# Fewer zeroed rows ahead of the scatters, a hold on weight tiles, and a free bank for the last attention round

## The chip, the cores and the metric

The kernel runs on one core of one Trainium2 chip. The metric is device time in microseconds (us) of one execution, as the median of several runs. The core has five engines that run their own instruction streams and wait for one another through semaphores: TensorE (PE in the profile, with its weight loads as PEld), VectorE (DVE), ScalarE (ACT), GpSimd (POOL) and SyncE (SP, which here only issues DMAs). ACT and POOL issue DMAs too.

## The reference

Three layers follow one another on 1536 tokens of width 384, all in float32:

```
state, per head, over 768 time steps:
    y_t = r_t (state + (u k_t) v_t);  state = w * state + k_t v_t      # 2 x 8 heads of width 48
x = y as 1536 tokens x 384
expert_idx = argmax(x @ w_gate)            # 8 experts, at most 384 tokens each, in token order
out[i] = gate_w[i] * (relu(x[i] @ w1[e]) @ w2[e])      # w1[e]: 384 x 1024, w2[e]: 1024 x 384
return (sigmoid(x @ w_gate2) * (x @ w_val)) @ w_out    # width 1536 between
```

## The kernel before

**Stage 1, attention.** Eight rounds `s` (four head pairs of two batches) run on PE, DVE, ACT and POOL. Round s does the output sums of its last two token blocks, transposes its result, and prepares rounds s+1 to s+3. `y_in` and `y_own` add up a round's outputs in PSUM, `out_evac` copies them to SBUF on ACT, `out_tr` transposes them on PE, `out_x` takes the transposed tokens and the gate's logits. For round 7, `y_in` takes one PSUM tile of two banks and calls its halves y7[0] and y7[1].

**Stage 2, routing.** `r1a` to `r3c` find each token's expert and its rank in it, for batch 0 during rounds 3 to 5 and for batch 1 after round 7. `r3c` writes gate weights behind each token's row and has POOL scatter the rows by six indirect DMAs per batch into a DRAM buffer `xs_d`, 1536 rows per expert (L228). The kernel works on NB = 224 rows of an expert at a time, so rows behind an expert's count are read too and must be finite: `zinit` (L663) writes zeros from SBUF over the first 224 rows of all eight experts, three DMAs in round 3 and five in round 4, on SP's queue. The first weight tile `raw[0]` is made to wait for all eight (`zl`, L140), so that it doesn't compete with them. Expert 0's rows of batch 0 come back by `pre()`; the rest of expert 0 is picked out of SBUF by matmuls in `first()`.

**Stage 3, experts.** 64 steps i = 8e + f. `s1(e, f)` multiplies expert e's tokens by a slice of w1, `s2` by a slice of w2, three steps later. Weight tiles of 384 KB come by `fetch` on SP into five buffers `raw`; `bg` splits each into a rounded part `rh` (ACT, L151) and the rest `rl` (DVE, L153). `eload(e)` brings expert e's 224 rows from `xs_d`: expert 1 at i = 0 on POOL's queue, expert 2 at i = 9 and expert 3 at i = 15 on SP's, the others at f = 7. `escale(e)` scales them on ACT (L939), `etr` transposes them on PE (L948). For expert 1 that is at i = 7 and 8, for expert e > 1 at f = 3 and f = 4, 6 of the expert before. `c1` (i = 9) sums the experts' counts on PE and DVE; `c3` loads offsets into registers. `dfetch` brings the tiles of stage 4's weights, 768 KB each, on SP.

**Stage 4**, the gated layer, is 48 steps of matmuls on the sorted tokens; its results are scattered to the output.

The order on every engine is the order in which the code calls these functions. Every engine, and the queue of DMAs that it issues, goes in order: an instruction that waits holds what is behind it. DMAs carry semaphores in rotation, eight for those of SP (DMAHW0 to 7) and eight for those of POOL (DMASW0 to 7), and a DMA also waits until the last one with its own semaphore has landed.

Of the kernel before, what the change touches and what calls it, by code (L numbers as in the profile page):

```python
# [32 lines left out]
WG = 5  # L33
ZI = (0, 0, 0, 3, 5, 0, 0, 0)
NKR = 3
# [79 lines left out]
def body(tc, A, out):  # L115
    nc = tc.nc
    E = mybir.EngineType
    with ExitStack() as top, tc.manual_schedule():
        gp_ = top.enter_context(tc.tile_pool(name="gp", bufs=1))
        rp_ = top.enter_context(tc.tile_pool(name="rp", bufs=NRAW))  # L120
        dr = top.enter_context(tc.tile_pool(name="dr", bufs=1, space=DRAM))
        xs_d = dr.tile([8 * 1536, XW], F32, tag="xs_d", name="xs_d")
        ids_d = dr.tile([1536, 1], I32, tag="ids_d", name="ids_d")
# [9 lines left out]
        def fetch(n):  # L133
            while nxt[0] < n:
                m = nxt[0]
                nxt[0] += 1
                raw[m] = rpl[0].tile([128, 768], F32, tag="raw", name="raw", bufs=rpl[1])
                i = nc.sync.dma_start(out=raw[m], in_=A["wx"][m // 2][:, (m % 2) * 768:(m % 2) * 768 + 768])
                if m == 0 or m == sum(BG) + 1:
                    after(i, xr0l if m else zl)  # L140

# [82 lines left out]

        scx, sci, sco, xr0l, zl = [], [], [], [], []

# [30 lines left out]
        mxi = gp_.tile([1, 1], I32, tag="mxi", name="mxi")  # L257
        one8 = gp_.tile([128, 8], F32, tag="one8", name="one8")
        cpos = gp_.tile([128, 12], I32, tag="cpos", name="cpos")
        with ExitStack() as ctx:  # L260
# [185 lines left out]
            def y_in(s):  # L446
                if s == 7:
                    y7t = ps.tile([128, 2, 512], F32, tag="a", name="y7")
                    for g in range(2):
                        y7[g] = y7t[:, g, :]  # L450
                else:
                    Y0[s] = pb.tile([128, 512], F32, tag="big", name="y0")
                T1[s] = pb.tile([128, 512], F32, tag="big", name="t1")
                for c in ((1, 4, 5, 2, 3) if s == 7 else (1, 2, 3, 4, 5)):
                    t = ts[s % 2].rearrange("q (d c) -> q d c", c=5)[:, :, c - 1]
                    for h in range(2):
                        q = slice(64 * h, 64 * h + 48)
                        nc.tensor.matmul(y_out(s, c)[64 * h:64 * h + 64], t[q], D[s][q, 0, c * 128:(c + 1) * 128],
                                         start=c in (1, 4) or s == 7 and c == 2, stop=False, skip_group_check=True)
# [125 lines left out]
            def first():  # L585
# [27 lines left out]

                nc.vector.tensor_scalar(out=keep, in0=rank, scalar1=capf, scalar2=None, op0=ALU.is_lt)
                choose(0)
                for c in range(6):
                    low(c)
                    if c < 5:
                        choose(c + 1)
                    if c == 0:  # L620
                        r3c(1)
                xk = [pb.tile([128, 512], F32, tag="big", name="xk")[:, 0:NB] for _ in range(3)]
# [29 lines left out]
            def consts():  # L652
# [6 lines left out]
                nc.gpsimd.tensor_copy(out=capf, in_=capi)  # L659

            zi = [0]

            def zinit():  # L663
                e = zi[0]
                if e < 8:
                    zi[0] += 1
                    zl.append(nc.sync.dma_start(out=xs_d[e * 1536:e * 1536 + NB, :].rearrange("(b p) d -> p b d", p=NP),
                                                in_=zero[0:NP]).ins)

# [66 lines left out]
            for s in range(8):  # L736
# [7 lines left out]
                fetch(sum(BG[:max(s + 2, 4)]) if s else 0)  # L744
                for _ in range(ZI[s]):
                    zinit()
                if s == 2:
# [10 lines left out]
                if nx:  # L758
# [3 lines left out]
                    if s == 6:  # L762
                        bg(1, False, 0, None, nc.vector.tensor_copy)
                    out_x(s, s == 6)
# [20 lines left out]
                if s == 6:  # L785
                    a_cp(7, C1, ap1)
                    bg(BG[s] - 2, False, 0, subs)
                    bg(1, False, 0, subs, nc.vector.tensor_copy)
                    cnt(0)
                    for f in subs:  # L790
                        f()
                if nx:
                    y_in(s + 1)
# [40 lines left out]
        with ExitStack() as ctx:  # L834
# [6 lines left out]
            def c1():  # L841
# [90 lines left out]
            def eload(e, eng=nc.sync):  # L932
                xr[e] = mp.tile([128, 2, XW], F32, tag="xr", name="xr")
                after(eng.dma_start(out=xr[e][0:NP], in_=xs_d[e * 1536:e * 1536 + NB, :].rearrange("(b p) d -> p b d", p=NP)), scx)

# [67 lines left out]
            for i in range(64 + LAG):  # L1003
                if i == OVP:
                    overflow()
                if i < 64:
# [142 lines left out]
```

## Time and profile before

| | |
|---|---|
| median of 3 runs | 452.23 us (450.78 to 454.71) |
| the profiled execution | 452.19 us, of which the instructions span 450.4 |
| PE busy | 432.6 us, 96% of the span |
| DVE, ACT, POOL busy | 63%, 50%, 24% |
| TensorE's granted clock, mean | 0.988 of full speed |

The profile counts an engine as busy while an instruction runs; a matmul's end is modelled, so that a busy PE is not PE at its peak. Waits are put down to the engine or DMA that released them last. Line numbers are those of the kernel before.

### The profile page before, as it was taken

How to read it: one execution, taken by the hardware profiler on the slowest of the kernel's cores; microseconds unless marked ns; L12 is line 12 of the kernel's file. 1: busy time of each engine (PE TensorE's matmuls, PEld its weight loads, DVE VectorE, ACT ScalarE, POOL GpSimd, SP SyncE). 2: the span in 40 equal slices, each digit the busy share in tenths (PEclk: the TensorE clock that was granted, in tenths of full speed). 3: DMA queues.
4: the chain of work that ended last, by engine and by line, in shares of the span. 5: the costliest groups of instructions: out<-in, count | busy, mean ns of one | idle time of the engine just before them, and what ended most of it. 6: DMA issues, size and time to landing. Idle time of an engine off the chain costs nothing.

```text
span 450.4 us, 8284 instructions
## 1 busy us (share of the span) xinstructions
PE 432.6 (96%) x3214; PEld 413.1 (92%) x3215; DVE 283.7 (63%) x496; ACT 224.3 (50%) x489; POOL 106.0 (24%) x102
## 2 busy tenths in 40 slices
PE   8999988969999999999999999999999999999994
PEld 4788876959999999999999999999999999999993
DVE  6888978727899899984677877778531222212211
ACT  5587765627787778763544444344352212222132
POOL 2466753300010112030035453232122000000013
PEclk9999999979999999999999999999999999999998
DMA  7999976754988886775026352340011000000002
GB/s 241 332 276 236 307 260 209 265 165 146 332 284 251 281 277 191 229 139 179 0 71 140 72 140 87 124 141 1 1 53 54 1 1 0 1 0 1 1 17 87
DMA packets 23194, 63.02 MB, mean 140 GB/s; under 512 B 4656, under 2 KB 8400, under 8 KB 23152
## 3 DMA queue, kind: packets, MB, share of 16 engines
q1 hardware_dynamic: 20992, 57.36, 43.0%
q0 software_dynamic: 2016, 5.10, 3.1%
q8 instruction: 26, 0.43, 0.4%
q14 instruction: 16, 0.13, 0.1%
q10 hardware_dynamic: 144, 0.00, 0.0%
HBM read 54.92 MB, written 7.53 MB: 139 GB/s over the span
## 4 chain that ended last, share of the span: by engine, by line
PE 72%; DMA 16%; ACT 4%; DVE 3%; issue 2%; POOL 1%; SPq 1%; POOLq 0%; DVEq 0%; ACTq 0%
PE pg L1072 17%; PE pv L1072 16%; PE po L1097 16%; PE ph L966 8%; PE py L985 7%; PE py L984 4%; DMA xs_d<-zero 4%; DMA kt<-in_kr_dram 3%; DMA raw<-in_wx_dram 3%; DMA dm<-in_dm_dram 3%; ACT rh L151 2%; DMA xr<-xs_d 1%; DMA xs_d<-xs,pi 1%; PE xp L948 1%; ACT xr L939 1%
## 5 line engine op out<-in xcount | busy, mean ns | idle before, releaser
L1082 DVE TENSOR_TENSOR sg<-sg,pv 128x384 f32<-128x384 f32 (+2 forms) x49 | 26.6, 543 | 79.5 <-PE pv L1072 79.5
L153 DVE TENSOR_TENSOR rl<-raw,rh 128x768 fp32r<-128x768 f32 x61 | 61.2, 1004 | 15.1 <-ACT rh L151 14.9
L985 PE MATMUL py<-hh,rh 128*128 128x448 f32 x192 | 65.1, 381 | 0.0
L1083 ACT CAST gh<-sg 128x384 fp32r<-128x384 f32 (+2 forms) x49 | 24.8, 507 | 78.1 <-DVE sg L1082 78.0
L1084 DVE TENSOR_TENSOR gl<-sg,gh 128x384 fp32r<-128x384 f32 (+2 forms) x49 | 35.6, 727 | 28.9 <-ACT gh L1083 28.9
L984 PE MATMUL py<-hh,rl 128*128 128x224 f32 x192 | 53.4, 278 | 0.0
L197 POOL TENSOR_TENSOR wy<-wa,wy 128x768 fp32r<-128x768 f32 x10 | 19.9, 1992 | 140.1 <-ACT wy L193 140.1
L1078 ACT ACTIVATE sg<-pg 128x384 f32<-128x384 f32 x48 | 23.5, 490 | 58.8 <-PE pg L1072 58.6
L151 ACT CAST rh<-raw 128x768 fp32r<-128x768 f32 x62 | 51.4, 832 | 1.8 <-DMA raw<-in_wx_dram 1.8
L968 ACT ACTIVATE hh<-ph 128x224 fp32r<-128x224 f32 x64 | 22.9, 358 | 34.0 <-PE ph L966 33.7
L228 POOL DMA_INDIRECT out_dram<-ob,ids x12 | 11.7, 975 | 118.0 <-ACT ob L1104 115.6
L985 PEld LDWEIGHTS py<-hh,rh 128*128 128x128 f32 x192 | 37.1, 193 | 2.2
L984 PEld LDWEIGHTS py<-hh,rl 128*128 128x128 f32 x192 | 37.6, 196 | 0.0
L1097 PE MATMUL po<-wy,gh 128*128 128x384 f32 x144 | 36.7, 335 | 0.0
L969 DVE SCALAR_TENSOR_TENSOR hh<-ph,hh 128x224 fp32r<-128x224 f32 x64 | 24.6, 385 | 10.4 <-ACT hh L968 9.9
L413 ACT ACTIVATE at<-cst,dl 128x128 f32<-128x128 f32 x88 | 27.2, 389 | 5.7 <-DVE dl L399 4.8
L966 PE MATMUL ph<-xh,rh 128*128 128x224 f32 x96 | 26.4, 275 | 0.4 <-DVE hh L969 0.4
L966 PE MATMUL ph<-xl,rh 128*128 128x224 f32 x96 | 26.5, 276 | 0.0
L966 PE MATMUL ph<-xh,rl 128*128 128x224 f32 x96 | 26.3, 274 | 0.0
L966 PE MATMUL ph<-xeh,rh 128*128 128x224 f32 x96 | 26.1, 274 | 0.0
L966 PE MATMUL ph<-xeh,rl 128*128 128x224 f32 x96 | 26.1, 275 | 0.0
L1097 PEld LDWEIGHTS po<-wy,gh 128*128 128x128 f32 x144 | 26.0, 188 | 0.0
(206 smaller groups left out, 1188.2 us busy)
## 6 DMA issues: line engine op xcount, KB each, us to landing
raw<-in_wx_dram SPq DMA_DIRECT2D x64, 384.0 KB, 4.6
r<-in_wy_dram SPq DMA_DIRECT2D x18, 768.0 KB, 4.9
kt<-in_kr_dram SPq DMA_DIRECT2D x7, 576.0 KB, 10.1
dm<-in_dm_dram SPq DMA_DIRECT2D x5, 672.0 KB, 10.4
xs_d<-zero SPq DMA_DIRECT2D x8, 339.5 KB, 7.2
v<-in_v_dram SPq DMA_DIRECT2D x8, 288.0 KB, 10.8
xr<-xs_d SPq DMA_DIRECT2D x6, 339.5 KB, 7.4
dm<-in_dm_dram SPq DMA_DIRECT2D x6, 288.0 KB, 11.6
```

Of the source, the lines that this page charges most:

```text
L151: cast(out=h, in_=t)
L153: (nc.gpsimd if pool else nc.vector).tensor_sub(rl[n % NR], t, h.bitcast(F32))
L413: nc.scalar.mul(AT[s][:, j, :], ident, DL[s][:, j:j + 1])
L966: nc.tensor.matmul(ph, a[:, w], b[:, kt, :], start=(i == 0), stop=(i == 8))
L969: nc.vector.scalar_tensor_tensor(out=h[:, 1, :], in0=ph, scalar=0.0, in1=h[:, 0, :].bitcast(F32), op0=ALU.max, op1=ALU.subtract)
L984: nc.tensor.matmul(y[:, 0, :], wl[:, w], h[:, 0, :], start=(f == 0), stop=False, skip_group_check=True)
L985: nc.tensor.matmul(y, wh[:, w], h, start=False, stop=(f == 7), skip_group_check=True)
L1072: nc.tensor.matmul(pg[g], w[a][:, q], x[b][:, kt, :], start=(kt == 0 and (a, b) == (0, 0)), stop=(kt == 2 and b == 1))
L1082: nc.vector.tensor_mul(gg[:, a:b], sg[:, a:b], pg[1][:, a:b])
L1083: nc.scalar.copy(out=gh[:, a:b], in_=gg[:, a:b])
L1084: nc.vector.tensor_sub(gl[:, a:b], gg[:, a:b], gh[:, a:b].bitcast(F32))
L1097: nc.tensor.matmul(po[i], g[v][:, a], w[u][:, q], start=(f == 0 and (u, v) == (0, 0)), stop=(f == 11 and v == 1))
```

## The change

- **Zeros.** `zinit` is gone. In round 3 four DMAs write zeros: over the rows of experts 0, 1 and 2, and into a new DRAM buffer `z_d` of 224 rows. Each of 112 partitions now writes two rows that lie together. `raw[0]` waits for no zeros.
- **Clearing later.** `c1` works out, for each expert whose count n is under 224, the row 1536e + n, else a row behind the buffer (which is 224 rows longer). At steps 11, 12, 13, 14 and 16 `clear(e)` for e = 3 to 7 loads that row into a register of POOL and copies `z_d` there, DRAM to DRAM, on POOL's queue.
- **Raw tiles held.** The tile with m = XG = 9 waits until expert 1's rows have landed (`xr1l`).
- **Round 7.** y7[1] is the bank that held the `ups` sums, so the two halves lie in two tiles. In round 6 all four of the round's `raw` casts stand ahead of `out_x` (one on DVE, three on ACT, where it was two and two), and the first subtraction with them.
- **`r3c(1)`** stands ahead of the first `choose`, no longer behind the second.

```
-        xs_d = dr.tile([8 * 1536, XW], F32, tag="xs_d", name="xs_d")
+        xs_d = dr.tile([8 * 1536 + NB, XW], F32, tag="xs_d", name="xs_d")
+        z_d = dr.tile([NB, XW], F32, tag="z_d", name="z_d")
...
-                if m == 0 or m == sum(BG) + 1:
-                    after(i, xr0l if m else zl)
+                if m in (sum(BG) + 1, XG):
+                    after(i, xr1l if m == XG else xr0l)
...
-                    y7t = ps.tile([128, 2, 512], F32, tag="a", name="y7")
-                    for g in range(2):
-                        y7[g] = y7t[:, g, :]
+                    y7[0] = ps.tile([128, 2, 512], F32, tag="a", name="y7")[:, 0, :]
+                    y7[1] = ud_ps
...
+                r3c(1)
                 choose(0)
                 for c in range(6):
                     low(c)
                     if c < 5:
                         choose(c + 1)
-                    if c == 0:
-                        r3c(1)
...
-                for _ in range(ZI[s]):
-                    zinit()
+                if s == 3:
+                    for z in [xs_d[e * 1536:e * 1536 + NB, :] for e in range(ZS)] + [z_d]:
+                        nc.sync.dma_start(out=z.rearrange("(p b) d -> p b d", b=2), in_=zero[0:NP])
...
                     if s == 6:
-                        bg(1, False, 0, None, nc.vector.tensor_copy)
+                        bg(1, False, 0, subs, nc.vector.tensor_copy)
+                        bg(BG[s] - 1, False, 0, subs)
+                        subs.pop(0)()
                     out_x(s, s == 6)
...
                 if s == 6:
                     a_cp(7, C1, ap1)
-                    bg(BG[s] - 2, False, 0, subs)
-                    bg(1, False, 0, subs, nc.vector.tensor_copy)
-                    cnt(0)
                     for f in subs:
                         f()
+                    cnt(0)
...
+                nc.vector.scalar_tensor_tensor(out=zo, in0=cf[0:1, :], scalar=-12288.0, in1=e1536, op0=ALU.add, op1=ALU.add)
+                nc.vector.scalar_tensor_tensor(out=zo, in0=cf[0:1, :], scalar=float(NB), in1=zo, op0=ALU.is_lt, op1=ALU.mult)
+                nc.vector.tensor_scalar_add(zoi, zo, 12288.0)
                 nc.vector.reduce_max(out=mxi, in_=cf[0:1, :], axis=AX.X)
+
+            def clear(e):
+                r = nc.values_load(zoi[0:1, e:e + 1], engines=[E.Pool], min_val=0, max_val=8 * 1536,
+                                   skip_runtime_bounds_check_because="behind an expert's rows")
+                nc.gpsimd.dma_start(out=xs_d[bass.ds(r, NB), :], in_=z_d)
...
+                    if i in ZE:
+                        clear(ZE[i])
```

with `ZS = 3`, `ZE = {11: 3, 12: 4, 13: 5, 14: 6, 16: 7}` and `XG = 9`.

SP's queue from the last `v` tile of attention (round 4) to the first tiles of stage 3, before the change. `dm<-xs_d` is `pre()`:

```order
L302 DMA v<-in_v_dram 128x576 [waits DMAHW3_49,PE_49]
L667 DMA xs_d<-zero 112x2x388 [waits DMAHW4_49]
L667 DMA xs_d<-zero 112x2x388 [waits DMAHW5_49]
L667 DMA xs_d<-zero 112x2x388 [waits DMAHW6_49]
L667 DMA xs_d<-zero 112x2x388 [waits DMAHW7_49]
L667 DMA xs_d<-zero 112x2x388 [waits DMAHW0_49]
L138 DMA raw<-in_wx_dram 128x768 [waits DMAHW5_49,DMAHW4_49,DMAHW6_49,DMAHW2_49,DMAHW7_49,DMAHW1_49,DMAHW0_49]
L138 DMA raw<-in_wx_dram 128x768
L138 DMA raw<-in_wx_dram 128x768 [waits DMAHW3_49]
L138 DMA raw<-in_wx_dram 128x768 x2
L581 DMA dm_124<-xs_d 112x2x388 [waits DMASW3_49,DMASW2_49,DMASW4_49,DMASW1_49,DMASW5_49,DMASW0_49,DVE_49]
L138 DMA raw<-in_wx_dram 128x768 [waits DMAHW6_49,DMAHW1_49,DVE_49]
```

and in the changed kernel, from the same `v` tile on:

```order
L308 DMA v<-in_v_dram 128x576 [waits DMAHW4_49,PE_49]
L141 DMA raw<-in_wx_dram 128x768 [waits DMAHW5_49]
L141 DMA raw<-in_wx_dram 128x768 [waits DMAHW6_49]
L141 DMA raw<-in_wx_dram 128x768 [waits DMAHW7_49]
L141 DMA raw<-in_wx_dram 128x768 [waits DMAHW0_49]
L141 DMA raw<-in_wx_dram 128x768 [waits DMAHW1_49]
L586 DMA dm_127<-xs_d 112x2x388 [waits DMASW3_49,DMASW4_49,DMASW2_49,DMASW5_49,DMASW1_49,DMAHW2_49,DMASW0_49,DVE_49]
L141 DMA raw<-in_wx_dram 128x768 [waits DMAHW3_49,DMAHW5_49,DMAHW2_49,DVE_49]
L141 DMA raw<-in_wx_dram 128x768 [waits DMAHW6_49,DMAHW4_49,DVE_49]
L141 DMA raw<-in_wx_dram 128x768 [waits DMAHW7_49,DVE_49]
L141 DMA raw<-in_wx_dram 128x768 [waits DMAHW0_49,DVE_49]
L141 DMA raw<-in_wx_dram 128x768 [waits DMAHW1_49,DMASW4_49,DVE_49]
```

The five zeroing DMAs between `v` and the raw tiles are gone, with the first raw tile's wait for them, and the last row shown, tile 9, has a new wait: DMASW4 is the semaphore of expert 1's rows.

POOL's stream from the last scatters of batch 1 on, before. `xr<-xs_d` is expert 1's `eload`, `wy` the first decoded weight of stage 4:

```order
L228 DMA xs_d<-xs,pi 12288x388 [waits DMASW1_49,Activation_49]
L228 DMA xs_d<-xs,pi 12288x388 [waits DMASW2_49]
L228 DMA xs_d<-xs,pi 12288x388 [waits DMASW3_49]
L934 DMA xr<-xs_d 112x2x388 [waits DMASW3_49,DMASW2_49,DMASW4_49,DMASW1_49,DMASW5_49,DMASW0_49,DMASW6_49,DVE_49,DMASW7_49,PE_49,Activation_49]
L1019 TENSOR_LOAD mxi [waits DVE_49]
L197 TENSOR_TENSOR wy<-wa,wy 128x768 [waits DMAHW3_49,Activation_49]
```

and in the changed kernel, from that `eload` on:

```order
L938 DMA xr<-xs_d 112x2x388 [waits DMASW3_49,DMASW2_49,DMASW4_49,DMASW1_49,DMASW5_49,DMASW0_49,DMASW6_49,DVE_49,DMASW7_49,PE_49,Activation_49]
L852 TENSOR_LOAD zoi [waits DVE_49]
L854 ISA
L854 DMA xs_d<-z_d 16x5432 [waits DMAHW7_49,DMAHW3_49,DMASW4_49]
L852 TENSOR_LOAD zoi
L854 ISA
L854 DMA xs_d<-z_d 16x5432 [waits DMASW5_49]
L1026 TENSOR_LOAD mxi [waits DVE_49]
L852 TENSOR_LOAD zoi
L854 ISA
L854 DMA xs_d<-z_d 16x5432 [waits DMASW6_49]
L852 TENSOR_LOAD zoi
```

Clears stand behind the `eload`. The first waits for DMAHW7, which is expert 2's rows on SP's queue, and each of the next for the semaphore of the clear ahead of it (DMASW5, 6, and for the fourth DMASW7), since the program can't tell which rows a register names. The fourth and fifth follow the rows shown.

SP's queue around the fourth expert's rows (e = 3, the row `xr<-xs_d`; `r` is a tile of stage 4's weights), before:

```order
L138 DMA raw<-in_wx_dram 128x768 [waits DMAHW2_49,DVE_49]
L138 DMA raw<-in_wx_dram 128x768 [waits DMAHW4_49,DVE_49]
L165 DMA r_1668<-in_wy_dram 128x1536 [waits DMAHW3_49]
L934 DMA xr<-xs_d 112x2x388 [waits DMASW4_49,PE_49]
L138 DMA raw<-in_wx_dram 128x768 [waits DMAHW5_49,DVE_49]
```

and in the changed kernel:

```order
L141 DMA raw<-in_wx_dram 128x768 [waits DMAHW6_49,DVE_49]
L141 DMA raw<-in_wx_dram 128x768 [waits DMAHW0_49,DVE_49]
L168 DMA r_1686<-in_wy_dram 128x1536 [waits DMAHW7_49]
L938 DMA xr<-xs_d 112x2x388 [waits DMASW0_49,PE_49]
L141 DMA raw<-in_wx_dram 128x768 [waits DMAHW1_49,DVE_49]
```

DMASW4 was the semaphore of expert 1's `eload`; DMASW0 is that of the fourth clear, so the load waits until four clears have landed, and the raw tiles behind it with it.

## Rows read from the trace of the kernel before

**Rows 1.** The page's head.
```profile
span 450.4 us, 8284 instructions
```

**Rows 2.** Stretches, us: length; busy PE, PEld, DVE, ACT, POOL; PEclk; DMA share; GB/s.
```profile
64.00:70.00 6.00, 4.42 (x40) 3.02 (x36) 3.94 (x10) 2.92 (x8) 2.08 (x3) 1.00 0.71 263
...
96.00:103.00 7.00, 6.94 (x32) 6.24 (x33) 2.02 (x4) 2.51 (x6) 0.00 (x0) 0.61 0.33 106
...
112.00:124.00 12.00, 12.00 (x97) 11.76 (x95) 10.19 (x24) 8.68 (x18) 0.00 (x0) 1.00 1.00 328
...
300.00:440.00 140.00, 140.00 (x806) 140.00 (x805) 45.04 (x75) 40.06 (x80) 13.78 (x12) 1.00 0.06 17
```

**Rows 3.** PE's timeline: start us, us, line, what, count, idle before it and releaser.
```profile
65.62 0.66 PE L465 MATMUL y<-at,v 128*64 128x128 f32 x8 [1.40 <-ACT yt L475]
...
66.64 1.66 PE L482 MATMUL xp<-cat,yt 128*128 128x136 f32 x12
...
96.03 0.82 PE L948 MATMUL xp<-cst,xr 112*128 112x112 f32 x3 [4.17 <-ACT xr L939]
...
98.67 0.82 PE L948 MATMUL xp<-cst,xr 112*128 112x112 f32 x3
```

**Rows 4.** DVE's timeline.
```profile
65.96 0.56 DVE L151 CAST rh<-raw 128x768 fp32r<-128x768 f32 x1 [2.13 <-DMA raw<-in_wx_dram]
...
69.19 0.26 DVE L507 TENSOR_TENSOR lg<-lg,xp 128x24 f32<-128x24 f32 x2
...
73.16 0.24 DVE L574 SCALAR_TENSOR_TENSOR xs<-rank,capf,se 128x24 f32<-128x24 f32 x1
```

**Rows 5.** The chain that ended last: start us, us, what.
```profile
50.48 7.24 DMA xs_d<-zero
...
81.44 6.40 DMA xs_d<-xs,pi
...
88.88 6.46 DMA xr<-xs_d
...
101.28 1.15 PE ph L966 x9
```

**Rows 6.** SP's timeline: DMA issues.
```profile
57.74 3.11 SPq L138 DMA_DIRECT2D raw<-in_wx_dram  x5
...
114.53 0.39 SPq L934 DMA_DIRECT2D xr<-xs_d  x1
```

**Rows 7.** POOL's timeline.
```profile
58.81 1.27 POOL L228 DMA_INDIRECT xs_d<-xs,pi  x1 [2.60 <-DVE at L437]
...
74.27 1.41 POOL L228 DMA_INDIRECT xs_d<-xs,pi  x1 [2.12 <-DVE pick L606]
...
81.44 1.72 POOL L228 DMA_INDIRECT xs_d<-xs,pi  x1 [0.30 <-issue]
```

**Rows 8.** ACT's timeline.
```profile
63.72 1.58 ACT L151 CAST rh<-raw 128x768 fp32r<-128x768 f32 x2
...
95.37 1.12 ACT L939 ACTIVATE xr<-xr 112x384 f32<-112x384 f32 x2 [4.05 <-DMA xr<-xs_d]
...
123.61 1.12 ACT L939 ACTIVATE xr<-xr 112x384 f32<-112x384 f32 x2
```

**Rows 9.** The instructions on `xs_d`: time from issue to landing of their DMAs.
```profile
DMA to landing us min/median/max: 2.7/6.9/9.1
```

**Rows 10.** The page's DMA issues: KB each, median us to landing.
```profile
dm<-xs_d SPq DMA_DIRECT2D x1, 339.5 KB, 3.1
```

**Rows 11.** Raw tiles issued from 72 to 74 us: time to landing.
```profile
DMA to landing us min/median/max: 3.2/4.0/5.3
```

**Rows 12.** The page's groups: busy us, mean ns of one, idle before and releaser.
```profile
L968 ACT ACTIVATE hh<-ph 128x224 fp32r<-128x224 f32 x64 | 22.9, 358 | 34.0 <-PE ph L966 33.7
```

**Rows 13.** DVE's timeline, the counts in `c1`.
```profile
106.19 0.14 DVE L850 TENSOR_REDUCE mxi<-cf 1x1 int32<-1x8 f32 x1
```

**Rows 14.** POOL's register load in step 13: duration ns min/median/max, start us.
```profile
L1019 POOLq TENSOR_LOAD <-mxi x1: 501/501/501, 106.4 to 106.4; - x1
```

More of the change, by code (lines that the diff above doesn't have):

```diff
@@ L33 @@
 WG = 5
-ZI = (0, 0, 0, 3, 5, 0, 0, 0)
+ZS = 3
+ZE = {11: 3, 12: 4, 13: 5, 14: 6, 16: 7}
+XG = 9
 NKR = 3
@@ L223, in tick @@
                         last = n
-        scx, sci, sco, xr0l, zl = [], [], [], [], []
+        scx, sci, sco, xr0l, xr1l = [], [], [], [], []
         def scatter(done, group, dst, index, src, rows):
@@ L258, in body @@
         one8 = gp_.tile([128, 8], F32, tag="one8", name="one8")
+        zo = gp_.tile([1, 8], F32, tag="zo", name="zo")
+        zoi = gp_.tile([1, 8], I32, tag="zoi", name="zoi")
+        e1536 = cst[0:1, 128 + 8 * OB:128 + 16 * OB].rearrange("o (e j) -> o e j", j=OB)[:, :, 0]
         cpos = gp_.tile([128, 12], I32, tag="cpos", name="cpos")
@@ L659, in consts @@
                 nc.gpsimd.tensor_copy(out=capf, in_=capi)
[L661 to L668, printed above, removed]
             def ok(q):
@@ L933, in eload @@
                 xr[e] = mp.tile([128, 2, XW], F32, tag="xr", name="xr")
-                after(eng.dma_start(out=xr[e][0:NP], in_=xs_d[e * 1536:e * 1536 + NB, :].rearrange("(b p) d -> p b d", p=NP)), scx)
+                i = eng.dma_start(out=xr[e][0:NP], in_=xs_d[e * 1536:e * 1536 + NB, :].rearrange("(b p) d -> p b d", p=NP))
+                after(i, scx)
+                if e == 1:
+                    xr1l.append(i.ins)
             def escale(e):
```

## Prediction

> **What bounds the kernel now.** The profiled execution took 452.19 us, 1.8 more than its span of 450.4 [rows 1], and the median of the runs shown is 452.23, so the sum is made against the span and 1.8 added. I read the stretches first: from 103 us on PE is busy nearly without a gap, as in 112 to 124 and 300 to 440, and at full clock [rows 2]. Nothing in the change takes matmuls out there. Time can be won only before, where PE's timeline shows two waits: 1.40 us at 65.6 in the last attention round, and 4.17 us at 96.0, for expert 1's rows [rows 3]. Behind the second one the granted clock of 96 to 103 is 0.61, so mostly the lower of its two levels, 1.2 of 2.4 GHz, while the wait of 1.40 left 64 to 70 at 1.00 [rows 2]. DVE's timeline adds a wait of 2.13 us for a raw tile at 66.0 [rows 4]. The chain that ended last runs through the same places: zeros landing at 50.48 + 7.24 = 57.72, a scatter from 81.44 to 87.84, expert 1's load from 88.88 to 95.34 [rows 5]. SP issues the first raw tile at 57.74, right behind the last zeros [rows 6].
>
> **Raw tiles earlier, and round 7.** SP's order shows the raw tiles in the places of five zeroing DMAs, so the fourth is issued where the last zeros were, at 50.48 [rows 5], and no longer from 57.74 on. Even at 9.1 us, the longest landing on `xs_d` [rows 9], it is there at 59.6, before DVE and ACT ask for it. On DVE the wait of 2.13 and the cast of about 0.5 (ACT now does it) go. On PE the wait of 1.40 goes, since the second half of round 7 no longer lies in the tile that ACT is emptying: the transposes end at 66.64 + 1.66 = 68.30 before [rows 3], and at 66.9 after. ACT's third cast (1.58 / 2 = 0.79 [rows 8]) fits into its wait for DVE's logits ahead of `out_x`. The last logits row on DVE, which ends at 69.19 + 0.26 = 69.45 [rows 4], needs the transposes and the three subtractions. The first are there at 66.9, the second at 69.2 - 2.1 - 0.5 = 66.6, so it ends at about 67.15. **Gain 2.3 us**, and the whole routing chain behind it moves by this. A smaller DMA load in rounds 4 to 6 I cost at nothing: no engine waits for a DMA there.
>
> **Expert 1's rows earlier.** POOL starts the first scatter of batch 0 at 58.81 [rows 7], 1.1 us behind the last zeros. Without that wait it follows the row indices, about 1.7 us earlier, so `pre()` is also back in time. For batch 1, `r3c` on DVE stood at 73.16 and ended at 73.40 [rows 4], and the first scatter started 0.87 later, at 74.27 [rows 7]. Ahead of `choose` it ends at about 69.9 on the new time axis, and the first scatter starts at 70.8. `choose` is moved back by 0.24, which the next rows give back, one `r3c` less between them. Six scatters take 81.44 - 74.27 = 7.2 to the last one's start [rows 7]: 78.0. Its landing took 6.40 beside five raw tiles [rows 5]. Tile 9 and those behind it are now held, so I take 2.7, the least on this buffer [rows 9]: 80.7. Then 1.04 to the load's issue, as from 87.84 to 88.88, and instead of 6.46 [rows 5] the 3.1 us of `pre()`'s load, of the same size on a quiet queue [rows 10]: the rows are there at 84.8 instead of 95.3.
>
> They are not used at 84.8, for the hold has a price. Tile 9's cast is due on ACT at step 5, at about 85.0, ahead of `escale(1)`. It is issued at 84.85 and lands 3.2 later, as the first of a burst did [rows 11]: 88.1. Behind it on ACT stand its cast, that of tile 10 and two Relus of 0.36 [rows 12], overlapping a little: 2.2 us. So `escale(1)` starts at 90.3 instead of 95.37 [rows 8], **5.1 us earlier**, 2.3 of them from above. PE, which was free at 91.86 and is now at 89.6, waits 1.3 us. That is near the 1.40 behind which the clock stayed at 1.00 [rows 2], so I take full clock. From the second transposes at 98.67 [rows 3] to the next expert's first matmuls at 101.28 [rows 5] lie 2.6 us of work at the lower clock. At the higher one DVE's half of the operand bounds it at about 1.6: **1.0 more. Gain until here 6.1 us.**
>
> **What the clears cost.** Three short DVE rows in `c1` like the one of 0.14 [rows 13] add about 0.5 us where DVE has slack. The five clears take POOL's time, which nothing needs until the first decoded weight. But they make a chain. On the old time axis the row numbers are ready at 106.3 + 0.5 = 106.8, the register load takes 0.5 [rows 14], issuing about 0.8, as in front of the scatters: first clear at 108.1. Expert 2's rows, which it also waits for, are there by then. Each of the next three waits for the clear ahead of it, 0.7 from landing to issue. Expert 3's load waits for the fourth, and SP with it. It was issued at 114.53 [rows 6], and ACT used the rows at 123.61 with no wait shown [rows 8], PE being fully busy: there is no slack. With L for a clear's time to landing and 3.1 for the load on a queue that has run empty [rows 10], the stall is 108.1 + 4L + 2.1 + 3.1 - 123.6 = 4L - 10.3 us, on whatever axis.
>
> No DMA from DRAM to DRAM is in the trace. From below the scatter's 2.7 bounds L [rows 9], with fewer bytes: 0.5 us of stall. From above the 6.46 of expert 1's load on POOL's queue beside raw tiles [rows 5]: 15.5 us. Nearest is 3.1 [rows 10], the same bytes, but the first two clears run while SP still issues (112 to 124 has a DMA share of 1.00 [rows 2]), the last two while SP stands still. I take 3.3: **3 us of stall**, between the two waits seen, so half of a slow stretch's price of about 1 us: 0.5. The tiles behind the load come in a burst, one per us, and ACT needs one per step; nothing is added. The fifth clear has the time of eight steps.
>
> The Trainium skill ("DMA: Bandwidth & Descriptors", section "Anatomy of one DMA — SWDGE (gpsimd) path") gives 2.0 us plus bytes / 436e3 for a DMA on POOL's queue. By it L would be an estimated 2.8, the stall 0.9 and the time about 447; the row of 3.1 is used instead.
>
> **Sum.** 450.4 - 6.1 + 3.0 + 0.5 = 447.8, plus 1.8: **449.5 us.**
>
> **Rivals.**
>
> *The clears are in time.* If L is 2.7 or less, expert 3's load is issued where SP gets to it and the whole 6.1 stands: 450.4 - 6.1 + 1.8 = 446, or 446.6 with the 0.5 at L = 2.7. For it: a clear has only 16 long descriptors, so little to write for POOL. Against it: the load needs four landings in a row, and no DMA in the trace landed in under 2.7.
>
> *Slow clears.* A copy that reads and writes DRAM may take longer than any one-sided row: at L = 4 the stall is 5.7. PE then idles longer than the 4.17 behind which the clock fell, and a PE-bound stretch at 0.61 costs more than in 96 to 103, where ACT and DVE shared the bound: 7 us at that rate deliver 2.7 less. 450.4 - 6.1 + 5.7 + 2.7 + 1.8 = 454.5. The sign turns at about L = 3.5 (stall 3.7 and up to 2.7), and at L = 4.6 it is slower by 1%: 457. For it: DMAs on POOL's queue beside raw tiles took 6.4 and 6.46 [rows 5]. Against it: a single descriptor per engine has to take turns with the raw tiles' packets only once.
>
> The skill has a rule for this: the same page's section "Latency and other measured facts" has copies between HBM tensors at 207 to 214 GB/s per direction; the section "Bandwidth" has loads of 425. An estimate by it puts some 0.8 us on L, about 3.9 and 454. No run so far shows it.
>
> *The hold costs what it gives.* If expert 1's load doesn't get faster without raw tiles beside it (6.46 again), `escale(1)` waits until about 93.6 behind tiles 9 and 10, PE idles for more than 4 us and the clock falls as before. The early gain is then 1.8, and with the clears' 3.5 the time is 450.4 - 1.8 + 3.5 + 1.8 = 454. Against it: the median and least landings, 6.9 and 2.7, differ by load.
>
> **Chances.** In time 0.18, the forecast (L from 2.7 to 3.5) 0.45, slow clears 0.29, the hold 0.08. The range takes the first two and most of the third: 445.5 to 456; the forecast's own is 446.6 to 452. A difference under 1% (4.5 us) is what a measurement of this kernel can't tell from none. Faster by over 1%, under 447.7, is the first case and a quarter of the second: 0.30. Slower, over 456.8, needs L above 4.6: 0.10. Within 1%: 0.60.
>
> **What would show it.** In the new profile: raw tiles issued before 52; no wait of DVE for raw at 64; PE's transposes ending near 66.9; first scatter of batch 1 near 71 and expert 1's load landing near 85; ACT waiting for tile 9 up to 88, `escale(1)` near 90.3; clock 1.00 behind it. Then four clears 0.7 us behind one another's landing, SP idle in front of expert 3's load, and ACT and PE waiting for that load some 3 us at about 117 to 121. A wait much longer or none there makes the forecast wrong by 4L, and a half clock behind it by up to 2.7 more.

## The result and the profile after

The changed kernel takes 458.79 us (458.45 to 459.18), the kernel before in the same comparison 453.08 (450.78 to 454.71): 1.013 times as long, with a 95% interval of 1.008 to 1.018. The forecast was 449.5, with a range up to 456. The profiled execution spans 456.8 us, against 450.4 [rows 1].

Stretches of the changed kernel (columns as in [rows 2]):

```profile
64.00:70.00 6.00, 5.88 (x59) 3.94 (x56) 5.12 (x19) 3.66 (x10) 1.65 (x2) 1.00 0.39 127
92.00:96.00 4.00, 3.48 (x16) 2.88 (x15) 1.96 (x5) 1.73 (x4) 0.00 (x0) 0.55 0.94 329
96.00:103.00 7.00, 7.00 (x48) 6.85 (x47) 3.39 (x12) 3.83 (x9) 0.00 (x0) 0.77 0.29 87
112.00:124.00 12.00, 8.87 (x70) 8.50 (x69) 9.07 (x17) 6.42 (x13) 0.97 (x2) 0.96 0.62 242
124.00:130.00 6.00, 2.89 (x11) 2.76 (x12) 1.68 (x2) 2.42 (x5) 0.49 (x1) 0.50 0.99 331
```

From 112 to 124 PE is busy for 8.87 us, where it was busy for all 12 before [rows 2], and from 124 to 130 it runs at the lower clock (0.50). The timeline of the changed kernel, engines picked out (start, length, engine and line, idle time ahead and its releaser):

```profile
66.96 0.18 DVE L512 TENSOR_TENSOR lg<-lg,xp 128x24 f32<-128x24 f32 x1 [0.41 <-PE xp L487]
...
71.36 1.05 POOL L231 DMA_INDIRECT xs_d<-xs,pi  x1 [1.46 <-ACT dg L608]
...
78.54 0.98 POOL L231 DMA_INDIRECT xs_d<-xs,pi  x1 [0.31 <-issue]
82.31 0.76 POOL L938 DMA_DIRECT2D xr<-xs_d  x1 [2.79 <-DVE rl L156]
...
89.04 0.83 ACT L154 CAST rh<-raw 128x768 fp32r<-128x768 f32 x1 [4.04 <-DMA raw<-in_wx_dram]
...
91.12 1.11 ACT L946 ACTIVATE xr<-xr 112x384 f32<-112x384 f32 x2
...
91.78 0.51 PE L955 MATMUL xp<-cst,xr 112*128 112x112 f32 x3 [2.34 <-ACT xr L946]
...
94.41 0.82 PE L955 MATMUL xp<-cst,xr 112*128 112x112 f32 x3 [0.53 <-DVE xl L959]
...
104.77 0.54 POOL L854 DMA_DIRECT2D xs_d<-z_d  x1 [21.71 <-DVE hh L976]
110.53 0.49 POOL L854 DMA_DIRECT2D xs_d<-z_d  x1 [5.23 <-DMA xs_d<-z_d]
116.65 0.49 POOL L854 DMA_DIRECT2D xs_d<-z_d  x1 [5.63 <-DMA xs_d<-z_d]
120.06 0.49 POOL L854 DMA_DIRECT2D xs_d<-z_d  x1 [2.92 <-DMA xs_d<-z_d]
...
123.12 0.33 SPq L938 DMA_DIRECT2D xr<-xs_d  x1
...
126.45 1.12 ACT L946 ACTIVATE xr<-xr 112x384 f32<-112x384 f32 x2 [6.19 <-DMA xr<-xs_d]
...
130.23 0.83 ACT L154 CAST rh<-raw 128x768 fp32r<-128x768 f32 x1 [1.36 <-DMA raw<-in_wx_dram]
```

Read downwards, it shows the three parts. The logits row ends at 67.14 instead of 69.45 [rows 4]. Expert 1's first transposes start at 91.78 instead of 96.03 and its second ones at 94.41 instead of 98.67 [rows 3], but behind a wait of ACT for tile 9 (4.04) and a wait of PE (2.34), and at a mean clock of 0.55 from 92 to 96. The expectations below call the transposes behind PE's wait "the second"; the waits of 4.17 and 2.34 stand ahead of the first. The four clears ahead of expert 3's load go one behind the other, and ACT waits 6.19 us for expert 3's rows. SP issues nothing between 110.52 and 123.12.

A yardstick for what follows: the time from ACT's Relu of one expert step to that of another. Early waits don't touch it, so it prices one place at a time. "5 to 8" holds expert 1's rows, "19 to 22" expert 3's, "27 to 30" expert 4's. Undisturbed they take 10.22, 6.49 and 6.49 us. In the kernel before the first took 15.41, from 87.06 to 102.47 on ACT's timeline:

```profile
87.06 0.36 ACT L968 ACTIVATE hh<-ph 128x224 fp32r<-128x224 f32 x1 [0.86 <-PE ph L966]
...
102.47 0.36 ACT L968 ACTIVATE hh<-ph 128x224 fp32r<-128x224 f32 x1 [2.50 <-PE ph L966]
```

So **5.19 us are all that can be had at expert 1's rows**: the 4.17 of PE's wait [rows 3] and 1.0 of half clock.

### The profile page after: what moved, and what is told of

Its sections match the earlier page's. It is cut to its first block, busy times and chain, and to the rows that moved or that the text cites. A ratio compares the mean times of both kernels' runs of the same rounds, so it can differ in the third digit from the quotient of the medians.

```text
span 456.8 us, 8304 instructions
## 1 busy us (share of the span) xinstructions
PE 435.9 (95%) x3212; PEld 417.1 (91%) x3215; DVE 283.4 (62%) x498; ACT 226.1 (49%) x490; POOL 108.4 (24%) x107
## 4 chain that ended last, share of the span: by engine, by line
PE 51%; issue 1%; POOL 1%; POOLq 0%; ACT 0%
PE pg L1081 17%; PE pv L1081 16%; PE po L1106 16%; PE py L992 1%; PE ph L973 1%; POOL out_dram L231 1%; PE py L991 1%; POOLq L1154 0%; ACT sg L1087 0%; POOLq L231 0%
## 5 line engine op out<-in xcount | busy, mean ns | idle before, releaser
L156 DVE TENSOR_TENSOR rl<-raw,rh 128x768 fp32r<-128x768 f32 x60 | 59.9, 1000 | 20.0 <-ACT rh L154 19.6
L992 PE MATMUL py<-hh,rh 128*128 128x448 f32 x192 | 66.5, 387 | 0.0
L991 PEld LDWEIGHTS py<-hh,rl 128*128 128x128 f32 x192 | 38.6, 201 | 0.0
L973 PE MATMUL ph<-xel,rh 128*128 128x224 f32 x96 | 26.4, 279 | 0.0
```

The costliest lines, as they stand in the source:

```text
L156: (nc.gpsimd if pool else nc.vector).tensor_sub(rl[n % NR], t, h.bitcast(F32))
L973: nc.tensor.matmul(ph, a[:, w], b[:, kt, :], start=(i == 0), stop=(i == 8))
L991: nc.tensor.matmul(y[:, 0, :], wl[:, w], h[:, 0, :], start=(f == 0), stop=False, skip_group_check=True)
L992: nc.tensor.matmul(y, wh[:, w], h, start=False, stop=(f == 7), skip_group_check=True)
```

## The experiments

The runs e1 to e4 share a chip and their runs of the kernel before, as do c0 and e5 to e7, e8 to e11, e12 to e15, and e16 with e17; the kernel before took 455.40, 456.57, 456.45, 453.06 and 452.51 us there. Yardstick times, in us, are from each run's one profile; for c0, e1 and e12 that is the slowest of the run's executions, for e9 the fastest.

| run | ratio to before (95%) | 5 to 8 | 19 to 22 | 27 to 30 |
|---|---|---|---|---|
| before | | 15.41 | 6.49 | 6.49 |
| changed | 1.013 (1.008–1.018) | 14.32 | 15.56 | 6.48 |
| e1 no clears | 0.998 (0.994–1.001) | 14.29 | 7.22 | 6.48 |
| e2 clears unchained | 1.008 (1.004–1.012) | 11.80 | 10.68 | 6.48 |
| e3 no hold | 1.011 (1.007–1.014) | 10.22 | 14.39 | 6.48 |
| e4 late clears, unchained | 0.997 (0.993–1.001) | 12.45 | 6.48 | 6.48 |
| c0 changed, again | 1.012 (1.007–1.017) | 13.56 | 16.18 | 6.48 |
| e5 no clears, no hold | 0.988 (0.984–0.992) | 10.22 | 6.95 | 6.48 |
| e6 before + hold | 1.004 (1.001–1.007) | 18.80 | 6.49 | 6.49 |
| e7 late clears, no hold | 0.990 (0.985–0.995) | 10.22 | 7.17 | 6.50 |
| e8 before + scatters first | 0.990 (0.985–0.994) | 10.21 | 6.49 | 6.49 |
| e9 round-seven part alone | 1.006 (1.002–1.009) | 15.58 | 6.49 | 6.49 |
| e10 short clears, no hold | 1.000 (0.996–1.004) | 10.24 | 11.37 | 6.48 |
| e11 late clears, chained, no hold | 1.008 (1.005–1.012) | 10.22 | 6.48 | 13.77 |
| e12 before + raw tiles early | 0.990 (0.986–0.994) | 14.76 | 7.14 | 6.48 |
| e13 before + two banks | 0.994 (0.991–0.998) | 10.22 | 6.50 | 6.48 |
| e14 = e5 | 0.987 (0.983–0.991) | 10.22 | 6.49 | 6.48 |
| e15 = e8 | 0.988 (0.984–0.992) | 10.21 | 6.49 | 6.49 |
| e16 before + e12 + e13 | 0.989 (0.985–0.992) | 10.21 | 6.49 | 6.49 |
| e17 = e9 | 0.989 (0.985–0.992) | 11.71 | 6.49 | 6.48 |

### The clears: chain or bytes

e1 takes the clears out of the changed kernel and writes all zeros early.

```diff
-ZE = {11: 3, 12: 4, 13: 5, 14: 6, 16: 7}
+ZE = {}
...
-                if s == 3:
-                    for z in [xs_d[e * 1536:e * 1536 + NB, :] for e in range(ZS)] + [z_d]:
+                if s in (3, 4):
+                    for z in [xs_d[e * 1536:e * 1536 + NB, :] for e in (range(3) if s == 3 else range(3, 8))]:
```

> The clears are taken out of the changed kernel: the zeros of all eight experts are written early again (three in round 3, five in round 4), without the first raw tile waiting for them; the hold on tile 9, the two banks and the early casts stay. Theory A (the chain of clears alone eats the gain): the steps up to 19 keep the gain of about 3.4 us that the changed kernel shows against the kernel before, and nothing is lost at step 20, so 449 to 451 us, and the wait of ScalarE on expert 3's rows (6.19) is gone. Theory B (the hold and the early part are themselves worth nothing): 453 us or more, with expert 3's rows in time.

Measured: 0.998, and the wait for expert 3's rows is gone. So the clears cost some 1.4% with the hold in place (1.012 in c0, another comparison, against 0.998), but without them the kernel isn't at the 0.991 to 0.996 of theory A. Something else eats the early gain, as theory B said.

e2 keeps the clears and takes away the waits between them (their rows are apart); each load waits for its own clear and the newest one.

```diff
-nc.gpsimd.dma_start(out=xs_d[bass.ds(r, NB), :], in_=z_d)
+i = nc.gpsimd.dma_start(out=xs_d[bass.ds(r, NB), :], in_=z_d).ins
+if clr:
+    tc.declare_no_dep(i, group="clr", reason="each expert has rows of its own")
+tc.add_to_no_dep_group("clr", i)
+clr[e] = i
...
-after(i, scx)
+after(i, scx + ([clr[e]] if e in clr else []))
```

> The same five clears at the same places, with the same bytes, but none waits for the one ahead of it; each expert's load waits for its own clear and for the newest one issued. Theory A (waits between clears): four copies of 348 KB run side by side from about 105; expert 3's rows land between 115 and 119 instead of 126.4, ScalarE's wait of 6.19 falls under 2 us, and the time is 450 to 453 us. Theory C (the copies' traffic, not their chain): the four copies take the 16 engines from the raw tiles, so the load lands no earlier than 122 or ScalarE's casts wait for raw tiles instead, and the time stays at 456 us or more.

Measured: 1.008. The timeline of e2:

```profile
110.41 0.54 POOL L856 DMA_DIRECT2D xs_d<-z_d  x1 [19.70 <-DVE hh L982]
...
113.58 0.49 POOL L856 DMA_DIRECT2D xs_d<-z_d  x1 [0.43 <-issue]
...
121.14 0.33 SPq L944 DMA_DIRECT2D xr<-xs_d  x1
...
121.83 0.90 ACT L176 ACTIVATE wa<-r 128x768 f32<-128x768 f32 x1 [2.69 <-DMA r<-in_wy_dram]
...
129.18 1.12 ACT L952 ACTIVATE xr<-xr 112x384 f32<-112x384 f32 x2 [2.53 <-DMA xr<-xs_d]
```

All four copies are out within 3.2 us, and the load is issued 10.7 us behind the first instead of 18.4. But it lands 8.0 us later instead of 3.3. The copies are not what slows it: their packets end at about 120, ahead of its issue at 121.14, and in the kernel before, without any copies, the load issued at 114.53 [rows 6] took 8.8 us. The 3.3 was its time on a queue that the chain had run empty. What the copies slowed is a tile of stage 4, which landed 10.3 us behind its issue (the two tiles beside the changed kernel's clears took 7.2 and 8.2), and ACT now waits for it too. Both theories have a part: 19 to 22 falls from 15.56 to 10.68, not to 6.49.

e10 keeps the chain and takes the bytes away (28 rows each, one eighth); it has no hold and all zeros early.

```diff
-nc.gpsimd.dma_start(out=xs_d[bass.ds(r, NB), :], in_=z_d)
+nc.gpsimd.dma_start(out=xs_d[bass.ds(r, 28), :], in_=z_d[0:28, :])
```

> The early part without the hold, all zeros written early, and on top the five clears at their places and in their chain, but each of 28 rows (43,456 bytes) instead of 224: one eighth of the bytes, the same four waits ahead of expert 3's load. The short copies leave nothing out, since the rows are zero already. Theory C (bytes): each link takes under 2.5 us, expert 3's rows are waited for less than 1 us, 0.988 to 0.991. Theory A (each link costs its 3 us or more whatever its bytes): the load is issued 3 us late or more, 0.995 to 1.005.

The timeline of e10:

```profile
105.44 0.54 POOL L854 DMA_DIRECT2D xs_d<-z_d  x1 [18.20 <-DVE hh L976]
109.98 0.49 POOL L854 DMA_DIRECT2D xs_d<-z_d  x1 [4.00 <-DMA xs_d<-z_d]
115.16 0.49 POOL L854 DMA_DIRECT2D xs_d<-z_d  x1 [4.68 <-DMA xs_d<-z_d]
118.91 0.49 POOL L854 DMA_DIRECT2D xs_d<-z_d  x1 [3.27 <-DMA xs_d<-z_d]
...
120.93 0.33 SPq L938 DMA_DIRECT2D xr<-xs_d  x1
...
124.27 1.12 ACT L946 ACTIVATE xr<-xr 112x384 f32<-112x384 f32 x2 [3.35 <-DMA xr<-xs_d]
```

Measured: 1.000, against 0.988 for the same kernel without clears (e5). From issue to issue the four links take 4.54, 5.18, 3.75 and 2.02 us, 15.5 together; with all the bytes it was 5.76, 6.12, 3.41 and 3.06, 18.4. An eighth of the bytes saves a sixth of the chain. Beside weight tiles in flight a link took 3.4 us or more with either size; only the last, with SP silent, is short (2.02 and 3.06).

Two runs put four of the clears behind expert 3's load, with expert 3's zeros written early: e4 (with the hold) and e7 (without) unchained, e11 (without) chained.

```diff
-ZS = 3
-ZE = {11: 3, 12: 4, 13: 5, 14: 6, 16: 7}
+ZS = 4
+ZE = {16: 4, 17: 5, 18: 6, 19: 7}
```

> Zeros for four experts early instead of three, and the other four cleared after expert 3's load, none waiting for the one ahead of it. Theory A: expert 3's load no longer stands behind any clear and is issued at about 112, the wait of 6.19 is gone; the four copies start when its rows have landed (about 115) and have some 12 us until expert 4's load: 449 to 452 us. Theory C (the traffic itself): the copies at 115 to 125 make raw tiles late there, ScalarE waits for raw tiles 3 us or more between 115 and 130, and the time is 453 to 456 us.

> Four experts' zeros early and the other four cleared behind expert 3's load, without the hold (this was 0.990 with copies side by side), now each clear waiting for the one ahead of it. In that run the clears began at 125.3 and expert 4's rows were wanted at 141.0, so its load has to be issued by some 135. Theory A (the chain): four links of 3.1 to 5.8 us end at 138 to 148, ScalarE waits 3 us or more for expert 4's rows, 0.997 to 1.010. Theory C (only the place in the traffic counts): 0.988 to 0.993, with no wait.

Measured: e4 0.997, the same as without clears (e1). e11 1.008, against e7's 0.990: there the four links take 18.5 us, expert 4's load waits, and 27 to 30 takes 13.77. The timeline of e11:

```profile
123.69 0.54 POOL L854 DMA_DIRECT2D xs_d<-z_d  x1 [34.19 <-DMA xr<-xs_d]
...
142.15 0.33 SPq L938 DMA_DIRECT2D xr<-xs_d  x1
...
145.33 1.12 ACT L946 ACTIVATE xr<-xr 112x384 f32<-112x384 f32 x2 [5.72 <-DMA xr<-xs_d]
```

So the chain costs in either place. The copies' traffic costs in the first place, where stage 4's tiles are due, and nothing that shows in the second.

### The hold

e3 takes the hold out of the changed kernel, e6 puts it alone into the kernel before, e7 is e4 without it.

```diff
-                if m in (sum(BG) + 1, XG):
-                    after(i, xr1l if m == XG else xr0l)
+                if m == sum(BG) + 1:
+                    after(i, xr0l)
```

> The changed kernel with raw tile 9 no longer held for expert 1's rows; all else as changed, the chain of clears too. Theory A (the hold gives): expert 1's rows land 1.5 to 3 us later than 85.9, TensorE's wait ahead of the second transposes (2.34) grows to 4 or more, and the time is 460 to 462 us. Theory D (the hold costs what it gives: ScalarE waited 4.04 us for tile 9): the wait of 4.04 falls under 2, the transposes at 91.78 move earlier by 1 us or more, and the time is 455 to 458 us.

> The hold alone, put into the kernel before: raw tile 9 waits until expert 1's rows have landed; zeros, banks and order as before. Theory A: expert 1's rows land some 4 us earlier than the 95.3 of before, and 1 to 4 us of it reach the end: 0.991 to 0.998. Theory D (tile 9 and the half clock take it back): 0.999 or more, with ScalarE waiting 3 us or more for tile 9.

> Four experts' zeros early, the other four cleared unchained behind expert 3's load (this was 0.997 with the hold), now without the hold on tile 9. Theory A (the hold is worth 1 to 4 us): 1.000 to 1.006. Theory D (the hold costs what it gives): 0.995 to 0.999, with TensorE's second transposes no later than with the hold.

Measured: e6 1.004, e7 0.990 against e4's 0.997. Both go theory D's way, e7 beyond the range that D gave. In the timeline of e6, tile 9's cast stands with its wait ahead of expert 1's scaling:

```profile
97.80 0.83 ACT L151 CAST rh<-raw 128x768 fp32r<-128x768 f32 x1 [7.40 <-DMA raw<-in_wx_dram]
...
99.92 1.11 ACT L942 ACTIVATE xr<-xr 112x384 f32<-112x384 f32 x2
...
100.58 0.82 PE L951 MATMUL xp<-cst,xr 112*128 112x112 f32 x3 [5.74 <-ACT xr L942]
```

And so it does in the timeline of e1, the changed kernel without clears:

```profile
96.54 0.83 ACT L154 CAST rh<-raw 128x768 fp32r<-128x768 f32 x1 [3.37 <-DMA raw<-in_wx_dram]
...
98.73 1.11 ACT L946 ACTIVATE xr<-xr 112x384 f32<-112x384 f32 x2
...
99.39 0.51 PE L955 MATMUL xp<-cst,xr 112*128 112x112 f32 x3 [1.78 <-ACT xr L946]
```

Without the hold, 5 to 8 takes 10.22 in every kernel that has the scatters first; with it 11.80 to 14.32. So it costs 1.6 to 4.1 us there, and 3.4 in the kernel before (18.80 against 15.41). What it gives is a shorter landing of expert 1's load, 3.59 us in the changed kernel against 5.98 and 6.39 in e14 and e15, but those rows are in time too.

In e3 the step is undisturbed as well, but the time is 1.011, not the 455 to 458 us of theory D; the chain's wait (6.33 us there) stays. Part of what hides the hold's 3 to 4 us may lie ahead of both yardsticks: in e3's profile, as in those of e1 and e2 beside it, the logits row ends at 75.1 to 75.5, 8 us later than in the changed kernel's first profile (67.14). The changed kernel itself was not run beside e3, and how much of e3's median this makes up is open.

### What gives the gain

c0 is the changed kernel again. e5 is its early part alone: no clears, no hold.

> The changed kernel once more, unaltered, so that the parts measured beside it share its chip and its runs of the kernel before. Every theory: 1.010 to 1.016 times the kernel before, as in the first comparison (1.013).

> The early part alone: the two banks, round seven's order and the first raw tiles without a wait for zeros; all eight experts' zeros written early, no clears, no hold on tile 9. Theory A (each part gives what the trace of the changed kernel shows ahead of its clears): the logits row comes 2.3 us earlier, so 0.993 to 0.997 times the kernel before. Theory B (the head's gain is taken back at expert 1's rows, which still come late, and by TensorE's half clock there): 0.998 to 1.003.

Measured: c0 1.012, e5 0.988, more than either theory gave. e8 has one edit in the kernel before, e9 all the rest of e5.

```diff
+                r3c(1)
                 choose(0)
                 for c in range(6):
                     low(c)
                     if c < 5:
                         choose(c + 1)
-                    if c == 0:
-                        r3c(1)
```

> The kernel before with one edit: the second batch's scatters are issued ahead of DVE's selections instead of behind the first of them. Theory E (this edit, not the hold, frees expert 1's rows from the raw tiles: the last scatter leaves ahead of the second group of raw tiles): TensorE's wait of 4.17 ahead of the second transposes is gone or under 1 us, and the time is 0.990 to 0.996. Theory F (the raw tiles and banks carry the early part's gain): 0.998 to 1.002, the wait stays above 3.

> The early part without that edit: two banks, casts and raw tiles early, zeros of all experts early, no hold, no clears; the scatters stand where they stood before. Theory E: the logits row is some 2.3 us earlier, but the wait ahead of the second transposes stays at 3 to 5 us: 0.995 to 0.999. Theory F: 0.988 to 0.991, as the whole early part gave 0.988.

Measured: e8 0.990, as theory E said; e9 1.006, above both ranges, with the wait of PE that theory E foretold (3.60). The one moved line is enough for the whole gain. The timeline of e15, the same kernel as e8:

```profile
81.73 0.98 POOL L228 DMA_INDIRECT xs_d<-xs,pi  x1 [0.30 <-issue]
85.38 0.75 POOL L933 DMA_DIRECT2D xr<-xs_d  x1 [2.67 <-DVE hh L968]
...
92.39 0.36 ACT L967 ACTIVATE hh<-ph 128x224 fp32r<-128x224 f32 x1 [0.86 <-PE ph L965]
92.64 1.11 ACT L938 ACTIVATE xr<-xr 112x384 f32<-112x384 f32 x2
...
93.30 0.51 PE L947 MATMUL xp<-cst,xr 112*128 112x112 f32 x3
...
98.71 0.36 ACT L967 ACTIVATE hh<-ph 128x224 fp32r<-128x224 f32 x1 [1.78 <-PE ph L965]
```

The next raw tile is issued at 83.77, 2.04 us behind the last scatter; before it was 0.90 (82.34 against 81.44 [rows 7]). Expert 1's load follows the last scatter by 3.65 us, not by 7.44. ACT's scaling and PE's first transposes wait for nothing.

Then the round-seven part, in halves (e12: the first lines of the diff, with the four casts ahead of `out_x` as in the change; e13: the last), in sum (e16, and e17 = e9 once more), and on top of the scatters (e14 beside e15).

```diff
-                if m == 0 or m == sum(BG) + 1:
-                    after(i, xr0l if m else zl)
+                if m == sum(BG) + 1:
+                    after(i, xr0l)
...
-                    y7t = ps.tile([128, 2, 512], F32, tag="a", name="y7")
-                    for g in range(2):
-                        y7[g] = y7t[:, g, :]
+                    y7[0] = ps.tile([128, 2, 512], F32, tag="a", name="y7")[:, 0, :]
+                    y7[1] = ud_ps
```

> One half of the round-seven part in the kernel before: the first raw tiles don't wait for the zeros, and their casts stand where the changed kernel has them; one bank for the sums, scatters, zeros and hold as before. Theory G (the prediction's step a: DVE's wait for a raw tile goes and the logits row comes 1 us or more earlier, and this reaches the end): 0.995 to 0.998. Theory H (it is given back at expert 1's rows, which still come late behind the scatters): 0.999 to 1.006.

> The other half alone: round seven's sums in two banks, all else as before. Theory G: TensorE's wait of 1.40 ahead of the last products falls by 1 us or more and the time is 0.996 to 0.998. Theory H: as with the raw tiles, the logits row comes earlier but the time is 0.999 to 1.003.

> The early part with the scatters first, no hold, no clears, once more, beside the scatters-first edit alone on the same chip (they were 0.988 and 0.990 in different comparisons). Theory G (the round-seven part adds 2.3 us to the edit): 0.983 to 0.987, and 0.004 or more under the other. Theory H (it adds nothing): 0.987 to 0.992, within 0.003 of the other.

> The kernel before with the scatters-first edit alone, once more: 0.987 to 0.993 by every theory; the comparison with the run beside it tells what the round-seven part adds.

> Both halves of the round-seven part put into the kernel before as they were measured alone (0.990 and 0.994), the zeros in the layout of before. Theory G (the two halves gain by themselves and add up at least in part): 0.984 to 0.990. Theory I (the halves gain only as they happen to move expert 1's scatters clear of the second group of raw tiles): anything from 0.988 to 1.006, and in the profile the wait ahead of the second transposes stands or falls with the last scatter's issue lying behind or ahead of those raw tiles.

> The same two halves in the changed kernel's layout of the zeros (112 runs of two rows) once more, which came out at 1.006. Theory J (the layout or the code around costs it): 1.003 to 1.008 again, 0.010 or more over the run beside it. Theory K (that comparison's chip, or chance): within 0.004 of the run beside it.

Measured: 0.990 and 0.994 alone, 0.989 for both, so they don't add up in full (0.989 lies in the ranges of theories G and I alike), and 0.987 against 0.988 on top of the scatters (theory H). e17 is at 0.989 where the same kernel, e9, had 1.006: theory K, not the layout of the zeros. In e16 and e17 the last scatter leaves early by itself (79.8 in e17), the load goes some 4.4 us behind it, and 5 to 8 takes 10.21 and 11.71; in e9 the load came 7.4 us behind it and the step took 15.58. e12's own profile (14.76) is of the slowest of its six runs, and doesn't explain its median; e9's is of the fastest of twelve, so 15.58 explains its 1.006 only in part.

So whatever brings the load close behind the last scatter collects most of the 5.19 us, once. Theories E and I put the delay down to the second group of raw tiles, but e6 speaks against that. There tile 9 is held: SP issues no raw tile between 75.35 and 94.70, the DMA engines' share is 0.27 and then 0.02 from 84 to 91, and still the load follows the last scatter by 6.58 us. The timelines of e6 on POOL and DVE:

```profile
84.42 1.71 POOL L228 DMA_INDIRECT xs_d<-xs,pi  x1 [0.30 <-issue]
91.00 0.75 POOL L934 DMA_DIRECT2D xr<-xs_d  x1 [4.86 <-DVE hh L972]
...
84.33 0.96 DVE L153 TENSOR_TENSOR rl<-raw,rh 128x768 fp32r<-128x768 f32 x1 [0.33 <-ACT rh L151]
```

Two stretches of e6, columns as in [rows 2]:

```profile
84.00:88.00 4.00, 4.00 (x35) 3.96 (x35) 3.67 (x7) 3.34 (x7) 1.83 (x2) 1.00 0.27 100
88.00:91.00 3.00, 3.00 (x24) 2.91 (x23) 2.44 (x4) 1.44 (x3) 0.00 (x0) 1.00 0.02 4
```

DVE's timeline of the kernel before has the same subtraction just ahead of the scatter of 81.44, which took 1.72 [rows 7]:

```profile
81.35 0.96 DVE L153 TENSOR_TENSOR rl<-raw,rh 128x768 fp32r<-128x768 f32 x1 [0.33 <-ACT rh L151]
```

Four profiles have the late load: the kernel before, e6, e9 and e12, with 6.58 to 7.48 us behind the last scatter. In all four this scatter takes 1.71 or 1.72 us on POOL, and DVE's first subtraction `rl` of the experts starts 0.09 or 0.10 us ahead of it. In the sixteen others the scatter takes 0.98, no `rl` starts just ahead of it, and the load follows in 3.65 to 4.46. So what the helpful edits share is that they shift the last scatter against DVE's work. That the overlap with `rl` is the cause was not tested by itself; the raw tiles account for at most the 0.9 us between e6 and the kernel before. What shifts e9 and e17, the same kernel, to either side was not settled.

The best versions are e14 (447.27 us, 0.987) and e15, which is the kernel before with one line moved (448.18 us, 0.988). Both beat the kernel before and the changed one.

## Why the prediction was wrong

**Raw tiles and round 7: right in this trace.** Raw tiles were issued from 48.27, the wait for raw was gone, and the logits row ended at 67.14 (predicted 67.15). It was not so everywhere: in the profiles of c0 and of e1 to e5, e7 and e9 to e11 the row ends at 70.28 to 75.50, in e6 and e8, which have the head of the kernel before, at 72.42 and 73.05. Where it does come earlier, in e14 against e15 (68.34 and 71.01), the medians differ by 0.9 us and the profiled executions by 2.1, with intervals of about 1.8 us either way. How much of the 2.3 us reaches the end is open.

**Expert 1's rows: the clock step failed, and the hold was given another edit's gain.** Predicted 6.1 us by Relu 8; measured 3.5 (98.95 against 102.47). The order of the waits was right: last scatter at 78.54, landing 2.7 us later, load landing at 85.90 (predicted 84.8), tile 9 held and cast at 89.04 (88.1), scaling at 91.12 (90.3). Of the missing 2.6 us, 0.8 are lost up to the scaling and 1.7 behind it. PE's wait was 2.34, not 1.3, and the step "I take full clock" failed: the granted clock of 92 to 96 is 0.55, and from the scaling to Relu 8 it took 7.83 us, 7.10 before, where the sum took off 1.0. The other fault is that the landing of 2.7 was given to the hold ("Tile 9 and those behind it are now held, so I take 2.7"). e15 has it without a hold (2.61), and e6 has the hold without it. The rival "the hold costs what it gives", at 0.08, was right in its name; its reason was not. The rows came fast, and the held tile's cast stood ahead of them on ACT.

**The clears: L mis-sized, mechanism right.** This is the step that turned the sign. The stall was to be 4L - 10.3, with L = 3.3 from `pre()`'s load on a quiet queue. The chain ran as told, but the first two clears landed 5.49 and 5.84 us behind their issue, beside the weight tiles, and the third 3.13; from the first clear to the load's issue it took 18.4 us, where 4 x 3.3 + 2.1 is 15.3. ACT's wait was 6.19, not 3. The half clock behind it (0.50 in 124 to 130) and the raw tiles that came in a burst (the 1.36 at 130.23) cost 2.9 more, not 0.5: 19 to 22 grew by 9.07. Thus -3.5 + 6.2 + 2.9 = +5.6, where the sum had -6.1 + 3.0 + 0.5 (as rounded, its terms make 449.6, not 449.5); 0.8 more comes later in the program. The rival "slow clears" (0.29) told the stall and the half clock. Its 457 for L = 4.6 is the nearest number in the text, but in part by luck: it holds an early gain of 6.1 and a stall of 8.1, both too large. The burst, which was to add nothing, is a term that it lacked too.

The price that the Trainium skill gives for a DMA on POOL's queue ("DMA: Bandwidth & Descriptors", section "Anatomy of one DMA — SWDGE (gpsimd) path") comes to an estimated 2.1 us for the short clears and 2.8 for the whole ones. The trace is near it for the links with SP silent (2.02 and 3.06); beside weight tiles they took 3.4 to 6.1. So here it held for a quiet queue alone, and the sum that was worked out by it, about 447, was farther off than the forecast.

**The chances.** Slower by over 1% had 0.10. All the errors had one sign: two waits priced without what followed them in the clock, a queue priced empty, and a cost of the hold priced too low.

## What to carry to other kernels

When several edits serve one wait, the wait's length is the most they can give together: find it in the profile (here 5.19 us) and try the cheapest edit alone. A hold on a load also holds whatever is behind that load's consumer on its in-order engine, so look what stands there before holding. Price a chain of dependent DMAs by landings beside the traffic that will be there, times the links. Here fewer bytes helped little, while moving the copies to where nothing is due, without the waits between them, took the whole cost away. And before a delay is put down to other traffic, look for a run in which that traffic is absent: here e6 showed the delay with the DMA engines nearly empty.

## What was not expected of the hardware

The same kernel ran up to the logits row in 67.14 us in the first comparison's profile and in 74.22 in c0's, the slowest of its six executions. In c0, all engines slow down from 60 to 66 us, the wait mostly charged to "issue" or to engines that had long been done, and then the granted clock is 0.50, the lower level. Stretches of c0:

```profile
60.00:62.00 2.00, 1.28 (x23) 0.91 (x18) 0.24 (x1) 1.15 (x4) 1.42 (x2) 1.00 0.39 147
62.00:64.00 2.00, 1.12 (x11) 0.88 (x7) 1.07 (x1) 0.00 (x0) 1.67 (x2) 1.00 0.48 185
64.00:66.00 2.00, 0.53 (x4) 0.33 (x4) 0.59 (x2) 0.50 (x2) 0.28 (x1) 0.92 0.30 113
66.00:72.00 6.00, 6.00 (x48) 5.30 (x48) 5.02 (x10) 3.42 (x7) 0.00 (x0) 0.50 0.49 143
```

PE's timeline of c0, a row where only "issue" is named:

```profile
63.85 0.60 PE L487 MATMUL xp<-cat,yt 128*128 128x136 f32 x3 [0.68 <-issue]
```

e8, which has the head of the kernel before, also loses time there: PE stands idle for 4.00 us ahead of 67.84, where it was 1.40 [rows 3], and the clock of 68 to 72 is 0.50. There the wait is put down to ACT and a raw tile, so it may not be the same thing. Nothing in the profile of c0 names a cause, and none was tried. It is why only ratios within one comparison, or the yardstick behind it, were used here.
